# A batched long convolution with top-128 experts: other occasions for the steps of the top-k search, and a first product one occasion later

## The chip, the cores and the metric

One core of a Trainium2 chip runs the whole kernel. The metric is device microseconds of one execution, lower is better; the kernel before takes 789.25 us, the median of three runs. TensorE (PE) multiplies matrices into PSUM, VectorE (DVE), ScalarE (ACT) and GpSimd (POOL) work on SBUF and, GpSimd excepted, on PSUM, and SyncE (SP) issues most DMAs. Each engine takes its own instructions in program order and waits for the others through semaphores.

## The reference

```python
# x: (8, 6336, 128), h: (6336, 128), w_gate: (128,), w1: (128, 1024), w2: (1024, 128), capacity = 128
L = 2 * S                                   # S = 6336, a full linear convolution along S
Xf = np.fft.rfft(x, n=L, axis=1)
Hf = np.fft.rfft(h, n=L, axis=0)
y = np.fft.irfft(Xf * Hf[None], n=L, axis=1)[:, :S, :]

scores = np.einsum('bsd,d->bs', y, w_gate)
out = y.copy()
for b in range(8):
    top = np.argpartition(-scores[b], 128)[:128]
    xe = y[b, top]
    ye = np.maximum(xe @ w1, 0.0) @ w2
    g = 1.0 / (1.0 + np.exp(-scores[b, top]))
    out[b, top] = y[b, top] + g[:, None] * ye
```

So there are two parts: a convolution of every channel over the sequence, and for each of the 8 batch rows the 128 positions with the largest score, to which a gated two-layer network is added.

## The kernel before

The convolution is a discrete Fourier transform written as matrix products. The work is cut into eight units (0 to 7); units 0 to 5 go in pairs (0/1, 2/3, 4/5), each unit of a pair holding half of the channels of two batch rows, and units 6 and 7 hold one batch row each. A unit passes four stages, and TensorE does the products of each:

- **a** (16 half blocks, `stage_a`, products at L194): the first transform of x, from blocks that a fold has prepared (L133, L134, on VectorE or GpSimd). ScalarE copies the results out (L211).
- **b** (13 steps, `stage_b`, products at L109): the second transform; VectorE multiplies the result twice by the filter's spectrum into place and into a tile `tx` (L276, L282), and GpSimd adds the halves (L287).
- **c** (16 steps, `stage_c`, products at L300): the first inverse transform, copied out by ScalarE (L301).
- **d** (8 steps, `stage_d`, products at L320), the last stage: the second inverse transform. ScalarE copies one half into a tile `st` (L324), VectorE makes the sums and differences there (L329, L330), GpSimd multiplies by the gate's weights into a tile `tm` (L338), VectorE reduces `tm` to scores (L356) and SyncE sends `st` to DRAM (L359). The last two belong to `rest`, which is issued one d step later.

Stage d's products go to three PSUM banks in turn, two a step, and stage c's to the same three.

The program is a list of steps, `plan`, written out in Python with no loop on the chip. Stretches of two kinds follow each other. In a **middle stretch** stage c of unit u alternates with stage b of unit u+1, two steps of each in turn. In a **last-stage stretch** stage a of unit u+2 alternates with stage d of unit u: a0 d0 a1 d1 ... a7 d7, eight rounds. In the profile they lie as follows (start of the stretch in us): c2/b3 266.5, a4/d2 319.1, c3/b4 348.8, a5/d3 402.4, c4/b5 431, a6/d4 483.4, c5/b6 512.6, a7/d5 566.9, c6/b7 596.9.

When both units of a pair have their scores, the 128 largest of each row have to be found. This is `search`, a generator. It first makes sortable keys in two parts (`keys`, L375 to L385; its scratch is the PSUM tile `spare`, called `pm` in the profile). Then come 11 rounds (5 for the keys' upper part, 6 for the lower). A round sets seven thresholds (L454), compares the keys with them (L464), counts (L466), and adds the counts of all partitions with a small TensorE product into `pm` (L109, `pm<-num,ones`); the next VectorE step reads the sums (L444, L446, L422) and goes on to the next thresholds. In middle stretches VectorE takes five of the seven thresholds and ScalarE the other two for each unit of the pair, as four sign operations (L470, L477); in last-stage stretches VectorE takes all seven (`share`). Between the two parts the keys are rewritten (L495 to L499). After the last round `places` finds the positions: marks on VectorE (L517 to L519), a first group of products, a copy (L549), a second group, a comparison step on VectorE (L562, L568), a third group of products, and an index step for each of the two units (L591 to L595).

A generator yields a letter for what it wants to do next: "v" or "l" for a VectorE step, "p" or "q" for products, "x" for whenever. `visit(kinds)` lets the search (`strands`) and then the place finding (`later`) go one step on if their letter is among `kinds`. These calls stand behind the steps of the plan:

- middle stretch, behind an odd b (and the last one): products ("pqx"); behind an odd c, for the first six of the eight groups: VectorE steps ("vlx").
- last-stage stretch, behind a2, a4 and a6: products; behind d0, d2 and d4: VectorE steps.

`st`, `tm`, `tx`, the comparison's `cmp` and the place finding's area `work` share five buffers of one size (`wide`, 128 x 1024 float32), taken in program order from those given back.

Of the kernel before, what the change touches and what calls it, by code (L numbers as in the profile page):

```python
# [33 lines left out]
def conv_moe(ctx, tc, x, h, w_gate, w1, w2, fa_d, wb_d, wc_d, at_d, tri_d, cst_d, outs):  # L34
# [143 lines left out]
    def products_a(unit, q, t):  # L178
        xs, es = blocks[(unit + 1) * 8 + q]
        tab = fah if unit < 0 else fa  # L180
        if (unit, q) == (1, 0):
            pt = freed[t]
        elif unit < 2:
            pt = turn(wheel)
        else:
            p = pair()
            pt = (p[:, 0:512], p[:, 512:1024], p)
        for j in range(4):
            for b in range(2):
                lanes = slice(b * 64, b * 64 + N1)  # L190
                for c in range(2):
                    w = xs[lanes, 2 * j + t, 0] if c else es[lanes, 2 * j + t]
                    o = pt[b][c * 64:c * 64 + 64, 0:400].rearrange("p (r j k) -> p r j k", r=2, j=4)[:, :, j]
                    nc.tensor.matmul(o, w, tab[lanes, c], start=True, stop=True)  # L194
        return pt

    def leave_a(unit, q, t, pt, engines):
        if unit < 0:
            dst = reg[1].rearrange("p (b r m t) -> p b r m t", b=2, r=2, t=2)[:, :, :, q * 200:q * 200 + 200, t]
        else:  # L200
            dst = reg[unit % 2].rearrange("p (h r b m t) -> p h b r m t", h=2, r=2, b=2, t=2)
            dst = dst[:, q // 4, :, :, q % 4 * 200:q % 4 * 200 + 200, t]
        if pt[2] is not None:
            ops = [(dst, pt[2].rearrange("p (b x) -> p b x", b=2)[:, :, 0:400].rearrange("p b (r m) -> p b r m", r=2))]
        else:
            ops = [(dst[:, b], pt[b][:, 0:400].rearrange("p (r m) -> p r m", r=2)) for b in range(2)]
        for e, (o, i) in zip(engines, ops):
            if e == "v":
                v.tensor_copy(out=o, in_=i)
            else:  # L210
                nc.scalar.copy(out=o, in_=i)  # L211
# [3 lines left out]
    def stage_a(unit, q, t):  # L215
        pt = products_a(unit, q, t)
        engines = "ss"
        if (unit, q) > (1, 4) and unit < 2 or unit == 0 and q > 2:
            engines = "sv" if pt[2] is None else "v" if pt[2] is pairs[0] else "s"
        held.append((unit, q, t, pt, engines))  # L220
        if unit < 2 or q != 4 or t:
            while held:
                leave_a(*held.pop(0))
# [169 lines left out]
    def search(units, paced):  # L393
# [30 lines left out]
        for part in range(2):  # L424
# [3 lines left out]
            for it in range(-1, levels[part]):  # L428
                unit = base ** (levels[part] - 1 - it)
# [31 lines left out]
                with nc.allow_low_precision("whole numbers up to 64"):  # L461
# [20 lines left out]
                    else:  # L482
                        signs()
                if paced:
                    yield "p"
                else:
                    if it >= 0:
                        lower(unit)
                    if part and it + 2 == levels[part]:
                        v.tensor_tensor(out=limits, in0=bb.broadcast_to([LN, 2]), in1=edges[0:LN], op=ALU.add)  # L490
                    if units[0] + 1 == NU:
                        mark[0] = num[0:LN, 0, 0:1]
                    yield "x"
# [283 lines left out]
    def visit(kinds="vlpqx", rest=True, of=None):  # L777
        for line in of or (strands, later, others)[:3 if rest else 2]:
            if line and asks.get(id(line), "x") in kinds:
                try:  # L780
                    asks[id(line)] = next(line[0]) or "x"
                except StopIteration:
                    line.pop(0)
                    asks.pop(id(line), None)

    def more():
        if others:
            next(others[0], None)
# [24 lines left out]
    for s in plan:  # L813
        kind, unit = s[0], s[1]
# [6 lines left out]
        if kind == "a":  # L821
            q, t = s[2:]
# [16 lines left out]
            if unit >= 2 and (q, t) == (0, 1):  # L839
                load_x(n + 7)  # L840
            if t:
                visit("pqx" if q and q % 2 == 0 else "x")
        elif kind == "j":
            c = s[2]
            if c == 6:
# [21 lines left out]
        elif kind == "b":  # L867
            stage_b(*s[1:], tabs.pop(s))
            if unit == SINGLE and s[2] in (9, 11):
                load_x((unit + 2) * 8 + s[2] // 2 + 1)  # L870
            visit("pqx" if s[2] % 2 or s[2] == 12 else "x")
        elif kind == "c":
            stage_c(*s[1:])
            i = HALVES.index(s[2] // 2 * 2)
            free = True
            if unit + 2 < NU and s[2] % 2:
                m = (unit + 3) * 8
                last = unit + 3 == NU
                for q in ((0,), () if last else (5,), (1,) if last else (6, 1), (4,), (2, 3), (), (), ())[i]:
                    load_x(m + q)  # L880
                q = (None, 0, None, None, 1, 4, 2, (3, 5))[i] if last else (None, 0, 5, 6, 1, 4, 2, 3)[i]
                free = i < 6
                for q in (q if isinstance(q, tuple) else () if q is None else (q,)):
                    fold(m + q, g if free or q == 5 else v)
            if unit + 1 == NU:
                for k in range(2):
                    if loaded[0] < 1:
                        load_w(loaded[0])
                        loaded[0] += 1
                if s[2] not in (4, 12):  # L890
                    visit("pq", False)
                    visit("vlx")
                if not later_half:
                    if count[0] < 4:
                        fetch()
                else:
                    if s[2] not in (0, 2, 8):
                        more()
                    if s[2]:
                        visit(of=(strands,))  # L900
            else:
                visit(("vlx" if free else "x") if s[2] % 2 else "x")
        elif kind == "d":
            busy[0] = unit + 1 == NU
            stage_d(*s[1:], tabs.pop(s))
            i = s[2]
            if unit + 2 < NU:
                visit("x" if i % 2 or i == 6 else "vlx")
            elif unit + 1 == NU:
                hold[0] = True  # L910
                visit()
        elif kind == "end":
            flush()
            busy[0] = False
            if unit == SINGLE:
                later_half.append(1)
                serial[0] = True
                while loaded[0] < 6:
                    load_w(loaded[0])
                    loaded[0] += 1  # L920
                others.append(experts())
            if unit >= SINGLE:
                strands.append(search([unit], False))
            elif unit % 2:
                strands.append(search([unit - 1, unit], True))
                if len(strands) == 1:
                    visit("x", False)
# [104 lines left out]
```

## Time and profile before

| | before |
| --- | --- |
| median of 3 runs (lowest, highest) | 789.25 us (788.64, 790.46) |
| the profiled execution, its span | 788.46 us, 786.7 us |
| TensorE matmul busy | 727.7 us, 93% of the span |
| TensorE weight loads busy | 631.0 us, 80% |
| VectorE busy | 632.2 us, 80% |
| GpSimd busy | 551.2 us, 70% |
| ScalarE busy | 449.7 us, 57% |
| mean granted TensorE clock | 0.991 |
| DMA | 157.64 MB, mean 200 GB/s |
| chain that ended last | PE 64%, DVE 18%, DMA 7%, issue 5%, ACT 3% |

Weight loads overlap matmuls, and matmuls are pipelined with modelled ends, so busy times of TensorE add up to a little more than its time. In the timeline rows below, the columns are start and length in us, engine, source line, operation, output and inputs with their shapes, and the count of instructions merged into the row; a bracket gives the time that the engine sat idle before the row and what ended it. Rows of one group that come from other places are parted by "...".

### The profile page before, as it was taken

The numbers are of one execution on the slowest core, as the hardware profiler recorded it, in microseconds if no ns is written. First come the engines' busy times: TensorE is split into PE (matmuls) and PEld (weight loads), VectorE is DVE, ScalarE is ACT, GpSimd is POOL, SyncE is SP. The second block draws the span as 40 slices with busy tenths as digits, with TensorE's granted clock in tenths as the row PEclk, the third lists the DMA queues.
The fourth block names the chain that finished last, engine by engine and source line by source line (L and its number), as shares of the span: only waits on it lengthen the run. The fifth ranks groups of instructions, "written<-read, shape, count | busy, mean of one in ns | idle before, by whom it ended". The sixth has DMA issues, their size and how long they took to land.

```text
span 786.7 us, 39709 instructions
## 1 busy us (share of the span) xinstructions
PE 727.7 (93%) x17566; PEld 631.0 (80%) x17566; DVE 632.2 (80%) x1070; ACT 449.7 (57%) x962; POOL 551.2 (70%) x406
## 2 busy tenths in 40 slices
PE   6799899999999999999999999999999998889565
PEld 6776688898889888888799789878988787879554
DVE  6579966767676799899777898999678997986883
ACT  5687653465346566665456566655554666666462
POOL 0039939976997599868977698767985676734823
PEclk9999999999999999999999999999999999999889
DMA  9539737567856775577647774699487846532600
GB/s 334 190 133 328 247 97 245 177 197 244 275 178 193 241 269 180 168 229 261 210 146 231 257 256 124 194 327 317 132 251 252 265 118 186 160 89 61 211 26 17
DMA packets 82293, 157.64 MB, mean 200 GB/s; under 512 B 9367, under 2 KB 30089, under 8 KB 82121
## 3 DMA queue, kind: packets, MB, share of 16 engines
q1 hardware_dynamic: 81224, 154.05, 60.7%
q8 instruction: 138, 2.26, 1.2%
q0 software_dynamic: 896, 1.05, 0.5%
q14 instruction: 35, 0.28, 0.1%
HBM read 121.77 MB, written 33.29 MB: 197 GB/s over the span
## 4 chain that ended last, share of the span: by engine, by line
PE 64%; DVE 18%; DMA 7%; issue 5%; ACT 3%; POOL 1%; SPq 1%; POOLq 0%; DVEq 0%; ACTq 0%
PE pb L300 22%; PE pt L109 17%; PE pt L194 10%; PE pb L320 10%; DMA out<-st 3%; DVE cmp L464 2%; PE pb L109 2%; ACT junk L477 2%; PE pb L194 2%; DVE tx L282 2%; DVE st L329 2%; DVE st L330 1%; DVE ss L354 1%; PE pm L109 1%; POOL tm L338 1%
## 5 line engine op out<-in xcount | busy, mean ns | idle before, releaser
L301 ACT COPY half<-pb 114x512 f32<-114x512 f32 x224 | 146.8, 655 | 166.0 <-PE pb L300 165.6
L287 POOL TENSOR_TENSOR big<-big,tx 128x512 f32<-128x512 f32 (+1 forms) x104 | 132.1, 1300 | 72.9 <-DVE tx L282 63.0
L338 POOL TENSOR_TENSOR tm<-st,wg 114x1024 f32<-114x1024 f32 x56 | 133.8, 2392 | 60.6 <-DVE st L330 41.9
L287 POOL TENSOR_TENSOR reg<-reg,tx 128x512 f32<-128x512 f32 (+1 forms) x104 | 130.9, 1292 | 43.8 <-PE pb L300 22.6
L300 PE MATMUL pb<-wc,reg 128*50 128x64 f32 x4096 | 123.1, 220 | 1.9 <-ACT st L324 1.9
L300 PEld LDWEIGHTS pb<-wc,reg 128*50 128x50 f32 x4096 | 119.2, 126 | 5.3 <-ACT st L324 2.6
L300 PEld LDWEIGHTS pb<-wc,big 128*50 128x50 f32 x4096 | 118.7, 126 | 3.0 <-ACT reg L211 0.2
L300 PE MATMUL pb<-wc,big 128*50 128x64 f32 x4096 | 120.9, 219 | 0.1
L320 PE MATMUL pb<-half,wbuf 114*50 114x128 f32 x1792 | 110.5, 273 | 3.3 <-DMA wbuf<-tab_at 1.4
L320 PEld LDWEIGHTS pb<-half,wbuf 114*50 114x50 f32 x1792 | 96.1, 122 | 9.5 <-DMA wbuf<-tab_at 1.6
L109 PE MATMUL pt<-big,wbuf 128*64 128x256 f32 x704 | 86.0, 388 | 0.1
L109 PE MATMUL pt<-reg,wbuf 128*64 128x256 f32 x704 | 85.1, 388 | 0.0
L211 ACT COPY reg<-pt 128x800 f32<-128x800 f32 x66 | 58.1, 929 | 37.4 <-PE pt L194 35.7
L282 DVE TENSOR_TENSOR tx<-pt,wbuf 128x1024 f32<-128x1024 f32 (+1 forms) x65 | 76.3, 1174 | 0.0
L329 DVE TENSOR_TENSOR st<-pb,st 114x512 f32<-114x512 f32 x56 | 38.6, 689 | 43.7 <-PE pb L320 29.2
L109 PEld LDWEIGHTS pt<-big,wbuf 128*64 128x64 f32 x704 | 51.1, 135 | 23.9 <-DVE tx L282 0.6
L109 PEld LDWEIGHTS pt<-reg,wbuf 128*64 128x64 f32 x704 | 53.1, 135 | 20.1
L356 DVE TENSOR_REDUCE ss<-tm 114x16 f32<-114x1024 f32 x48 | 58.4, 1216 | 7.9 <-POOL tm L338 7.4
L211 ACT COPY big<-pt 128x800 f32<-128x800 f32 x56 | 49.2, 934 | 24.6 <-PE pt L194 22.7
L194 PE MATMUL pt<-fa,big 50*64 50x100 f32 x2336 | 60.5, 250 | 1.0 <-issue 0.7
L282 DVE TENSOR_TENSOR reg<-pt,wbuf 128x1024 f32<-128x1024 f32 (+1 forms) x39 | 45.9, 1178 | 18.8 <-PE pt L109 18.5
L194 PEld LDWEIGHTS pt<-fa,big 50*64 50x64 f32 x2336 | 52.4, 133 | 7.8 <-issue 4.9
(177 smaller groups left out, 1197.9 us busy)
## 6 DMA issues: line engine op xcount, KB each, us to landing
wbuf<-tab_at SPq DMA_DIRECT2D x128, 200.0 KB
out<-st SPq DMA_DIRECT2D x112, 200.0 KB
wbuf<-tab_wb SPq DMA_DIRECT2D x84, 256.0 KB
wbuf<-hd SPq DMA_DIRECT2D x84, 256.0 KB
big<-in_x SPq DMA_DIRECT2D x37, 512.0 KB
half<-in_x SPq DMA_DIRECT2D x15, 512.0 KB
hd<-st SPq DMA_DIRECT2D x24, 256.0 KB
reg<-in_x SPq DMA_DIRECT2D x12, 512.0 KB
```

Of the source, the lines that this page charges most:

```text
L109: nc.tensor.matmul(out[lo:hi], w[:, lo:hi], r, **k)
L194: nc.tensor.matmul(o, w, tab[lanes, c], start=True, stop=True)
L211: nc.scalar.copy(out=o, in_=i)
L282: v.tensor_tensor(out=dst.rearrange("p h a j k t -> p k h a j t"), in0=src, in1=w, op=ALU.mult)
L287: g.tensor_tensor(out=yv[:, :, r], in0=yv[:, :, r], in1=zv[:, :, 1 - r], op=ALU.add if r else ALU.subtract)
L300: nc.tensor.matmul(pt[i2 * 64:i2 * 64 + N1, o:o + HD], w, wc[:, i2], start=True, stop=True)
L301: nc.scalar.copy(out=hv[0:LN, c * 4 + j:c * 4 + j + 2].rearrange("p j r m t -> p (j r) t m"), in_=pt[0:LN].rearrange("p (j t m) -> p j t m ...
L320: nc.tensor.matmul(pt[r][a * 64:a * 64 + N1, c * 128:c * 128 + 128], ats[c // 2][0:LN, c % 2, a, r], hv[0:LN, :, r, m], start=True, stop=True)
L329: v.tensor_tensor(out=st[:, 0:512], in0=pt[1][0:LN], in1=st[:, 512:1024], op=ALU.add)
L338: e.tensor_tensor(out=tm[:, o:o + z].rearrange("p (a d) -> p a d", d=n), in0=st[:, o:o + z].rearrange("p (a d) -> p a d", d=n), in1=w.unsq ...
L356: v.tensor_reduce(out=ss[u][:, :, :, 4 * i:4 * i + 4].rearrange("p b s c -> p s c b"), in_=tm.rearrange("p (s c b d) -> p s c b d", s=2, c ...
L464: v.tensor_tensor(out=cv, in0=cur.unsqueeze(2).broadcast_to([LN, nb, nv, HD]), in1=nth[:, :, 0:nv].unsqueeze(3).broadcast_to([LN, nb, nv, ...
```

## The change

The change touches four places. The condition in `stage_a` is rewritten. The search yields "p" once more, and so lets one occasion for a product pass, between its first comparison and its first product, for pairs 0/1 and 2/3 (`units[0] < 4`). The last-stage stretches offer other occasions: products behind a1, a4 and a7 in place of a2, a4 and a6, and VectorE steps behind d1 and d4 in place of d0, d2 and d4.

```diff
@@ stage_a
-        if (unit, q) > (1, 4) and unit < 2 or unit == 0 and q > 2:
+        if unit == 0 and q > 2 or unit == 1 and q > 4:
             engines = "sv" if pt[2] is None else "v" if pt[2] is pairs[0] else "s"
@@ search
                 if paced:
+                    if it < 0 and not part and units[0] < 4:
+                        yield "p"
                     yield "p"
@@ the plan's loop, stage a
             if t:
-                visit("pqx" if q and q % 2 == 0 else "x")
+                visit("pqx" if q in (1, 4, 7) else "x")
@@ the plan's loop, stage d
             if unit + 2 < NU:
-                visit("x" if i % 2 or i == 6 else "vlx")
+                visit("vlx" if i in (1, 4) else "x")
```

Followed through the plan, the steps of pair 0/1 come at these places (pair 2/3 does the same two units later, pair 4/5's own steps stay where they are):

| stretch | before | with the change |
| --- | --- | --- |
| c2/b3 | keys; comparisons 1 to 5; products 1 to 5, from b3 on | keys; comparisons 1 to 4; products 1 to 4, from b5 on |
| a4/d2 | d0: count and key rewrite; d2: comparison 6; a4: product 6; d4: count and comparison 7; a6: product 7 | d1: count and comparison 5; a4: product 5; d4: count and key rewrite |
| c3/b4 | comparisons 8 to 11, products 8 to 11; marks; first and second products of the place finding | comparisons 6 to 11, products 6 to 11 |
| a5/d3 | d0: comparison step; a2: third products; d2, d4: index steps | d1: last count and marks; a4: first products; d4: copy; a7: second products |
| c4/b5 | | c5: comparison step; b1: third products; c7, c13: index steps |

In the last row the search of pair 2/3 begins in the same stretch; for pair 2/3 that row is c6/b7, where the search of pair 4/5 begins.

## Rows read from the trace of the kernel before

**Rows 1.** Busy time by stretch: length, then busy us (instructions) of each engine, clock, DMA
```profile
158.60:186.30 27.70, 27.70 (x774) 25.30 (x776) 18.68 (x22) 19.07 (x25) 20.30 (x12) 1.00 0.71 215
...
319.10:348.80 29.70, 27.91 (x778) 25.43 (x780) 26.37 (x39) 18.90 (x25) 21.80 (x12) 1.00 0.69 207
```

**Rows 2.** Timeline, TensorE, search products: start, length, form, [idle before <-releaser]
```profile
281.79 0.20 PE L109 MATMUL pm<-num,ones 114*64 114x14 bf16 x2 [0.82 <-ACT junk L477]
...
343.38 0.20 PE L109 MATMUL pm<-num,ones 114*64 114x14 bf16 x2 [1.34 <-DVE num L466]
...
446.12 0.19 PE L109 MATMUL pm<-num,ones 114*64 114x14 bf16 x2 [0.86 <-ACT junk L477]
...
499.22 0.20 PE L109 MATMUL pm<-num,ones 114*64 114x14 bf16 x2 [0.53 <-DVE num L466]
...
507.18 0.19 PE L109 MATMUL pm<-num,ones 114*64 114x14 bf16 x2 [1.01 <-DVE num L466]
...
612.49 0.19 PE L109 MATMUL pm<-num,ones 114*64 114x14 bf16 x2 [1.12 <-ACT junk L477]
...
619.75 0.17 PE L109 MATMUL pm<-num,ones 114*64 114x14 bf16 x1
```

**Rows 3.** Timeline, VectorE, search operations inside the stretch of Rows 1's second row
```profile
323.96 0.17 DVE L444 TENSOR_TENSOR ge<-pm,least 114x14 f32<-114x14 f32 x1
...
324.88 1.72 DVE L497 TENSOR_SCALAR key<-key 114x128 f32<-114x128 f32 x1
326.63 0.23 DVE L498 TENSOR_SCALAR key<-key 114x128 f32<-114x128 f32 x1
...
327.11 0.68 DVE L329 TENSOR_TENSOR st<-pb,st 114x512 f32<-114x512 f32 x1
...
340.31 0.16 DVE L444 TENSOR_TENSOR ge<-pm,least 114x14 f32<-114x14 f32 x1
```

**Rows 4.** Timeline, GpSimd, the same stretch
```profile
328.64 4.85 POOL L338 TENSOR_TENSOR tm<-st,wg 114x1024 f32<-114x1024 f32 x2 [2.12 <-issue]
333.45 1.27 POOL L133 TENSOR_TENSOR big<-big 128x512 f32<-128x512 f32 x1
```

**Rows 5.** Timeline, TensorE and then VectorE, start of the stretch after 430.8 us
```profile
434.25 3.80 PE L109 MATMUL pt<-reg,wbuf 128*64 128x256 f32 x32
...
434.92 1.22 DVE L356 TENSOR_REDUCE ss<-tm 114x16 f32<-114x1024 f32 x1 [1.43 <-POOL tm L338]
...
437.83 0.43 DVE L385 TENSOR_TENSOR key<-pm,cst 114x256 f32<-114x256 int32 x1
```

**Rows 6.** Timeline, VectorE and then TensorE, place finding in the stretch 402 to 431
```profile
407.55 1.28 DVE L562 TENSOR_TENSOR work<-tri,pm 114x512 bf16<-114x512 f32 x2
408.75 0.75 DVE L568 SCALAR_TENSOR_TENSOR work<-pm,work 114x256 bf16<-114x256 f32 x2
...
416.83 0.15 DVE L591 TENSOR_SCALAR base<-pm 128x1 f32<-128x1 f32 x1
...
417.59 0.68 DVE L329 TENSOR_TENSOR st<-pb,st 114x512 f32<-114x512 f32 x1
...
411.00 0.29 PE L109 MATMUL pm<-lanes,work 114*64 114x1 bf16 x8
...
411.52 1.94 PE L320 MATMUL pb<-half,wbuf 114*50 114x128 f32 x32
```

**Rows 7.** Timeline, VectorE, one round of the stretch 597 to 650
```profile
630.35 0.16 DVE L444 TENSOR_TENSOR ge<-pm,least 114x14 f32<-114x14 f32 x1
...
632.82 0.68 DVE L276 TENSOR_TENSOR reg<-pt,wbuf 128x512 f32<-128x512 f32 x1
...
637.60 0.16 DVE L444 TENSOR_TENSOR ge<-pm,least 114x14 f32<-114x14 f32 x1
```

**Rows 8.** Timeline, ScalarE and then SyncE's queue, stretch 402 to 431
```profile
413.75 0.59 ACT L324 COPY st<-pb 114x512 f32<-114x512 f32 x1 [1.57 <-DMA out<-st]
...
407.94 1.69 SPq L359 DMA_DIRECT2D out<-st  x2
```

## The prediction

> **What bounds the kernel now.** I read the stretch table first. The middle of the kernel (158 to 650 us) repeats two kinds of stretch: last-stage stretches (first products of one unit beside the sums and output of another, eight rounds) and middle stretches (stages b and c). Where no search runs, TensorE is busy for the whole stretch, 27.70 of 27.70 us, which makes a round 3.46 us; the clock is full in both rows [rows 1]. So TensorE is the bound, and any other engine matters only where TensorE waits for it. With search steps beside it the same stretch takes 29.70 us, with TensorE busy for 27.91 and VectorE up from 18.68 to 26.37 [rows 1]. Then I listed TensorE's instructions and looked for idle brackets. Each pair's search has 11 counting products; [rows 2] has seven of the three pairs', six with an idle bracket. Two kinds: beside the last stage they wait for VectorE's counts (1.34, 0.53, 1.01 us), and the first one after a pair's keys waits for ScalarE's signs (0.82, 0.86, and 1.12 for the third pair) [rows 2]. All of it is 5.7 us, 0.7% of the span; a few smaller waits are left as they are. That is the purse the change can pay from.
>
> **The change, part by part.** The condition on `engines` is rewritten, and selects the same units and blocks: nothing. The rest moves steps; the number of products, counts and place-finding products is the same, so TensorE's own work is left out of the sum wherever it stands. For pairs 0/1 and 2/3 the last-stage stretch held three VectorE steps after d0, d2, d4 and products at a4, a6; it then holds two, after d1 and d4, and one product, at a4. What no longer fits moves on: six search rounds instead of four in the next middle stretch, place finding (marks, first and second products) beside the following last stage, and its third products and index steps into the middle stretch after that, where the next pair's search starts.
>
> (1) First product of pair 0/1, one occasion (7 us) later: its signs are long done, -0.8 us [rows 2].
>
> (2) First product of pair 2/3: -0.9 us [rows 2]. But the third products of pair 0/1 now stand just before it, after the second b. They write the bank in which the keys' halves lie, so they wait until VectorE has read those. The keys' last operation starts at 437.83 and lasts 0.43, TensorE's second b ends at about 437.9 (434.25 + 3.80, less the overlap of ends), so the bare wait is some 0.3 us [rows 5]. VectorE gets the comparison step of place finding (1.28 + 0.75 = 2.0 us) [rows 6] ahead of that, where it idled 1.43 us for GpSimd [rows 5], so the keys end some 0.65 us later: wait +0.95. Net +0.1; bounds -0.6 (wait 0.3) and +0.5.
>
> (3) Beside the last stage, twice. The waits of 1.34 and of 0.53 + 1.01 go: -2.9 us [rows 2]. What is late next is VectorE itself. A step with its count takes 3.0 us (from 340.31 until the product at 343.38) [rows 2, 3], a round's own VectorE work is two sums of 0.68 and a reduction of 1.2 [rows 3, 5]. Counted from the end E1 of d1 on TensorE: 0.2 of latency, sums, reduction and step end at E1+5.7, so d2's sums end at E1+7.1 instead of E1+5.0. GpSimd's multiply of d2 (2.42, half of 4.85) then ends at E1+9.5, the fold queued behind it (two operations of 1.3) at E1+12.1, the multiply of d3 at E1+14.5, which is E4+4.1 [rows 4]. The reduction of d3 waits for that, and the second step stands behind the reduction: it starts at E4+5.3. It contains the key rewrite, 3.15 us in all (323.96 to 327.11) [rows 3], so d5's sums end at E4+8.7 to +9.9. TensorE's d7 needs the bank that they free at E4+8.45, and the next stage's first and third blocks need the banks of d6 and d7. VectorE has 5.1 us more to do until the last of them, at E4+13.8 to +15.0, and TensorE wants it at E4+12.2. That makes 1.6 to 2.8 us of wait in each stretch; if d3's reduction isn't held up it is none. I take 1.5 each, +3.0, so part (3) is +0.1; bounds -2.9 and +2.7.
>
> What the rewrite costs decides within that. One of its operations takes 1.72 us and the next, of the same form, 0.23 [rows 3]. [...]
>
> (4) Start of pair 4/5's search, from 597 us. Its first product isn't moved, and the comparison step, third products and both index steps of pair 2/3 now come into it. There VectorE has no room: a round is a step of 2.47 and products of 4.78, together 7.25 [rows 7], which is TensorE's round too (612.49 to 619.75, and the second product has no wait) [rows 2]. An index step is 0.76 [rows 6]. Two of them and the 0.65 of part (2) put the third product 2.2 us later. TensorE fills 0.5 of that with the moved third products themselves (411.00 to 411.52) [rows 6], which are not counted: +1.65. Bounds +0.6 (the wait for the keys hides one index step) and +2.0.
>
> (5) Buffers. Outputs, products, comparisons and the place-finding work area share five buffers, taken in the order in which they were given back. The work area held one over d0 to d2 in the stretch shown; it then holds one from d1 until the next middle stretch. Where four were left, ScalarE's copy of d2 waited 1.57 us for the output of d0 to land, 5.8 us after its issue at 407.94 [rows 8]. A buffer then takes copy and sums 2.1 (0.59 + 2 x 0.68, issue), transfer 5.8, so 7.9 per two rounds of 6.9: up to 1 us of lag more every second round. TensorE first waits when the copy is some 2.8 us late (the bank that it frees is used again 0.95 into the next sums), which d6 or d7 could just reach. I take +0.5 in each of two stretches, nearest to the one row that shows no cost on TensorE, +1.0; bounds 0 and +4.
>
> (6) One comparison a pair goes from seven thresholds on VectorE to five there and four signs on ScalarE: nothing, since only a search's first product waits for signs there and the moved one is not a first [rows 2]; without that cover up to 1.1 us a pair, the largest such wait [rows 2]. No DMA is issued by a moved step, so SyncE's and GpSimd's queues keep their order.
>
> Sum: -0.8 + 0.1 + 0.1 + 1.65 + 1.0 = **+2.0 us**. The profiled execution took 788.46 us with a span of 786.7, so it would take 790.5. The median of the three runs shown is 0.8 above the profiled one, so the predicted time is 789.25 + 2.0 = 791.3 us.
>
> **Rivals.** *Buffers in full*: part (5) reaches +4. For it: the lag grows by itself once it starts; against it: only one copy in the row's stretch waited, and buffers may be handed over in a kinder order. 794.3 us. *Faster, the last stage runs clear*: with two steps in place of three VectorE has 3 us less to do there. If the step after d1 ends before GpSimd is pushed behind its fold, d3's reduction isn't held, no bank is late and outputs leave early enough for four buffers: parts (3) and (5) lose 3.0 and 1.0, 787.3 us. It decides at E1+5.0, the time at which d2's sums end undisturbed. For it: VectorE's total there falls below eight rounds; against it: the step is 3.0 us in one piece. *VectorE absorbs the index steps*, and buffers cost nothing: -1.65 - 1.0, 788.6 us; against it the 7.25 of 7.25. *It does not do what it says*: waits move without a net effect, 789.3 us.
>
> **How the numbers follow.** Chances: forecast 0.40 (own range 789.9 to 792.7), buffers in full 0.15, last stage clear 0.17, index steps absorbed 0.18, no effect 0.10. A difference of 0.2% (1.6 us) is about what a measurement of this kernel can tell from none, so the borders are 787.7 and 790.8. Faster: 0.17 and 0.02 of the absorbed case, 0.19. Same: the rest of that, 0.16, no effect 0.10, and 0.07 of the forecast below 790.8: 0.33. Slower: 0.33 + 0.15 = 0.48. The range runs from the clear case to the full buffers, 787.3 to 794.5.
>
> **What would show it.** Right: no idle bracket before the pair's first products; no product waiting beside the last stage, but waits of 0.2 to 1.5 us before the last sums there and the first blocks of the next stage; a wait of about 1 us before each group of third products; second and third products of pair 4/5 waiting 0.7 us each. It is wrong if VectorE is idle before the sums of d5, if the multiply of d3 starts on time, or if pair 4/5's products run without waits. Instruction fetch gaps on TensorE (0.3 to 0.5 us each, in stretches without search too) are left as they are; moved, they could shift the time by about as much.

## The result, and the profile after

The changed kernel takes 796.7 us, the median of 22 runs (792.0 to 802.3); the kernel before took 791.5 beside it (22 runs, 788.6 to 796.2), 2.3 us more than in the three runs known ahead. The ratio is 1.0055 (95% interval 1.0033 to 1.0078): slower by 4.4 us (2.6 to 6.2; the two medians lie 5.2 apart). The forecast was +2.0.

The profiled execution has a span of 794.1 us, 7.4 more than before. That is more than the medians differ, since the profiled execution of before (788.46) lies 3.1 us below the median of its 22 runs and that of after (795.91) 0.8 below its own. The stretch table shows where the 7.4 are: five stretches of before and then of after (c2/b3, a4/d2, c4/b5, a7/d5, c6/b7; length, then busy us and instructions of TensorE, its weight loads, VectorE, ScalarE, GpSimd, then clock, DMA share, GB/s).

```profile
266.30:319.00 52.70, 51.88 (x1240) 45.24 (x1234) 49.09 (x67) 30.08 (x77) 45.41 (x36) 1.00 0.67 218
319.00:348.50 29.50, 27.71 (x773) 25.22 (x772) 26.47 (x39) 18.84 (x25) 21.61 (x12) 1.00 0.69 206
430.60:483.40 52.80, 51.94 (x1244) 45.34 (x1238) 49.17 (x67) 30.04 (x76) 45.75 (x36) 1.00 0.67 220
566.80:596.67 29.87, 28.33 (x800) 25.60 (x800) 19.93 (x33) 18.99 (x25) 24.11 (x14) 1.00 0.69 211
596.67:650.50 53.83, 52.00 (x1241) 43.92 (x1237) 50.28 (x100) 30.77 (x78) 34.17 (x28) 1.00 0.68 213
```

```profile
266.80:318.40 51.60, 51.60 (x1238) 43.00 (x1232) 46.82 (x61) 28.17 (x67) 44.32 (x35) 1.00 0.66 218
318.40:346.70 28.30, 27.70 (x775) 25.04 (x771) 21.35 (x34) 19.09 (x25) 21.28 (x12) 1.00 0.68 206
428.60:483.90 55.30, 53.09 (x1274) 45.81 (x1268) 51.14 (x74) 28.85 (x69) 47.38 (x36) 1.00 0.64 208
566.30:597.73 31.43, 29.13 (x798) 26.14 (x798) 19.17 (x29) 18.43 (x24) 24.01 (x15) 1.00 0.64 195
597.73:657.30 59.57, 54.89 (x1272) 44.97 (x1268) 54.02 (x113) 31.10 (x78) 35.12 (x28) 0.97 0.62 195
```

The change gains where it takes steps away (c2/b3 -1.1, a4/d2 -1.2, with VectorE at 21.35 us there for 26.47) and loses where they go: c4/b5 +2.5, a7/d5 +1.6, and above all c6/b7, +5.7, where the clock's mean is 0.97.

At the start of c4/b5, TensorE's timeline (start, length, form, in brackets the idle time ahead and what ended it) shows two blocks of stage c waiting for the last stage's banks, and then the third products of pair 0/1 waiting for pair 2/3's keys:

```profile
428.68 1.06 PE L300 MATMUL pb<-wc,big 128*50 128x64 f32 x32
430.77 1.10 PE L300 MATMUL pb<-wc,big 128*50 128x64 f32 x32 [1.02 <-ACT st L324]
432.22 2.00 PE L300 MATMUL pb<-wc,big 128*50 128x64 f32 x64 [0.34 <-DVE st L330]
434.05 3.80 PE L109 MATMUL pt<-reg,wbuf 128*64 128x256 f32 x32
438.44 0.29 PE L109 MATMUL pm<-lanes,work 114*64 114x1 bf16 x8 [0.60 <-DVE key L385]
```

Inside c6/b7 the same two waits stand again, for pairs 2/3 and 4/5, and then comes a gap that no other engine ends:

```profile
599.64 1.10 PE L300 MATMUL pb<-wc,big 128*50 128x64 f32 x32 [0.75 <-ACT st L324]
601.09 2.00 PE L300 MATMUL pb<-wc,big 128*50 128x64 f32 x64 [0.34 <-DVE st L330]
...
607.32 0.29 PE L109 MATMUL pm<-lanes,work 114*64 114x1 bf16 x8 [0.61 <-DVE key L385]
...
613.26 0.55 PE L300 MATMUL pb<-wc,big 128*50 128x64 f32 x13 [2.01 <-issue]
613.64 3.40 PE L109 MATMUL pt<-reg,wbuf 128*64 128x256 f32 x16
...
618.88 0.17 PE L109 MATMUL pm<-num,ones 114*64 114x14 bf16 x2
```

"issue" means that TensorE waited for nothing that the profile shows. Behind it 16 products of stage b take 3.40 us in place of 2.0. The table of these microseconds shows two things: the DMA engines are full until 614 (a share of 1.04), and the granted clock is 0.50 from 614 to 616, after TensorE stood still for 2.01 us.

```profile
610.00:612.00 2.00, 1.24 (x45) 1.13 (x41) 2.00 (x4) 1.20 (x2) 2.00 (x2) 1.00 1.04 386
612.00:614.00 2.00, 0.74 (x17) 0.66 (x18) 1.89 (x5) 0.15 (x1) 2.00 (x3) 0.97 1.04 385
614.00:616.00 2.00, 2.00 (x14) 1.05 (x12) 0.82 (x5) 1.87 (x8) 0.81 (x1) 0.50 0.44 159
616.00:618.00 2.00, 2.00 (x16) 1.17 (x14) 0.92 (x2) 0.44 (x2) 0.00 (x0) 0.68 0.01 5
```

TensorE's instructions come by DMA too. The page's queue list (queue, kind, packets, MB, share) has

```profile
q8 instruction: 138, 2.26, 1.2%
```

and 2.26 MB in 138 packets are 16.4 KB each, which for 2 x 17566 products and weight loads is one packet for about 255 instructions. The places of the gaps give the size too. Counted in order of start, TensorE's semaphore instructions among them, the gaps marked "issue" after 100 us stand at instructions 3521, 3777, 11458, 11714 and 15298 in the profile of before, and at 3521, 3777, 11714, 21954, 23490 and 28865 in that of after: multiples of 256 apart, to within one. So one fetch brings a block of 256. Most borders between blocks show no gap: of the 126 packets of q8 that land after 99 us in each of the two profiles, only 5 and 6 are followed by such a gap; the one in the timeline above is 2.01 us.

That such a gap is a late fetch can be read from the trace. One packet of q8 runs from 610.83 to 612.03, the first since 603.04, and TensorE goes on at 613.26, 1.23 us after it has landed. All 11 gaps marked "issue" on TensorE after 100 us, in the profiles of both kernels, end 1.23 to 1.58 us after a packet of q8 has landed; in the runs below, gaps with this mark are counted as late fetches. The packet before the gap took 1.20 us, against a median of 1.07 for q8 in this execution: it was not slow, it came late.

The new steps beside the last stage ran as the prediction had them. VectorE and GpSimd in a4/d2 (timeline; the brackets as above), then TensorE at its end:

```profile
326.86 1.21 DVE L356 TENSOR_REDUCE ss<-tm 114x16 f32<-114x1024 f32 x1
...
339.87 1.22 DVE L356 TENSOR_REDUCE ss<-tm 114x16 f32<-114x1024 f32 x1 [2.29 <-POOL tm L338]
341.01 0.16 DVE L444 TENSOR_TENSOR ge<-pm,least 114x14 f32<-114x14 f32 x1
...
341.93 0.35 DVE L499 TENSOR_SCALAR key<-key 114x128 f32<-114x128 f32 x1
342.32 0.23 DVE L500 TENSOR_SCALAR key<-key 114x128 f32<-114x128 f32 x1
342.58 0.29 DVE L501 TENSOR_TENSOR key<-key 114x128 f32<-114x128 f32 x1
342.79 0.68 DVE L329 TENSOR_TENSOR st<-pb,st 114x512 f32<-114x512 f32 x1
```

```profile
334.84 1.29 POOL L133 TENSOR_TENSOR big<-big 128x512 f32<-128x512 f32 x1
336.20 1.29 POOL L134 TENSOR_TENSOR big<-big 128x512 f32<-128x512 f32 x1
337.45 4.75 POOL L338 TENSOR_TENSOR tm<-st,wg 114x1024 f32<-114x1024 f32 x2
```

```profile
346.69 2.00 PE L300 MATMUL pb<-wc,reg 128*50 128x64 f32 x64 [0.49 <-DVE st L330]
349.35 2.00 PE L300 MATMUL pb<-wc,reg 128*50 128x64 f32 x64 [0.66 <-DVE st L330]
```

No product of the search waits in a4/d2 or a6/d4 any more, against 2.9 us in [rows 2].

### The profile page after: what moved, and what is told of

The parts are those of the page before. It is cut to its first block, busy times and chain, and to the rows that moved or that the text cites. A ratio compares the mean times of both kernels' runs of the same rounds, so it can differ in the third digit from the quotient of the medians.

```text
span 794.1 us, 39720 instructions
## 1 busy us (share of the span) xinstructions
PE 732.3 (92%) x17566; PEld 629.8 (79%) x17566; DVE 628.0 (79%) x1070; ACT 453.3 (57%) x980; POOL 551.6 (69%) x406
## 3 DMA queue, kind: packets, MB, share of 16 engines
q8 instruction: 138, 2.26, 1.2%
## 4 chain that ended last, share of the span: by engine, by line
PE 64%; DVE 21%; issue 6%; DMA 5%; ACT 3%; SPq 1%; POOL 1%; POOLq 0%; DVEq 0%; ACTq 0%
PE pb L300 21%; PE pt L109 17%; PE pt L194 11%; PE pb L320 10%; DMA out<-st 3%; DVE cmp L464 2%; DVE tx L276 2%; PE pb L109 2%; PE pb L194 1%; DVE ss L354 1%; DVE st L329 1%; DVE st L330 1%; PE pm L109 1%; DVE big L276 1%; DVE tx L282 1%
## 5 line engine op out<-in xcount | busy, mean ns | idle before, releaser
L338 POOL TENSOR_TENSOR tm<-st,wg 114x1024 f32<-114x1024 f32 x56 | 133.8, 2393 | 63.5 <-DVE st L330 52.8
L109 PEld LDWEIGHTS pt<-reg,wbuf 128*64 128x64 f32 x704 | 50.6, 136 | 23.5 <-issue 1.0
```

The costliest lines, as they stand in the source:

```text
L109: nc.tensor.matmul(out[lo:hi], w[:, lo:hi], r, **k)
L338: e.tensor_tensor(out=tm[:, o:o + z].rearrange("p (a d) -> p a d", d=n), in0=st[:, o:o + z].rearrange("p (a d) -> p a d", d=n), in1=w.unsq ...
```

## The experiments

What had to be told apart: are the 4.4 us the waits that the prediction summed (buffers, keys, index steps), or the late instructions? Each run stands beside the kernel before on the same chip; its ratio is given with the 95% interval. Diffs are against the changed kernel unless said otherwise.

**Each pair alone.** The first-pair run keeps the old occasions for units 6 and 7 of stage a:

```diff
-visit("pqx" if q in (1, 4, 7) else "x")
+visit("pqx" if q in ((1, 4, 7) if unit < 6 else (2, 4, 6)) else "x")
-visit("vlx" if i in (1, 4) else "x")
+visit("vlx" if i in ((1, 4) if unit < 4 else (0, 2, 4)) else "x")
-if it < 0 and not part and units[0] < 4:
+if it < 0 and not part and units[0] < 2:
```

> The change for pair 0/1 alone: new occasions in the last-stage stretches a4/d2 and a5/d3 and the later first product for that pair; pair 2/3 keeps the old ones, so pair 4/5's search starts as in the kernel before. Theory A (the loss sits where pair 4/5's search starts, c6/b7, which took 59.5 us in place of 53.7, and in the stretch ahead of it, 31.5 in place of 30.0): no loss, ratio to before 0.998 to 1.001, c6/b7 53 to 55 us, and no gap of 2 us between TensorE's instructions there. Rival B (each pair pays by itself, for its keys, its index steps and its buffers): about half of the 4.4 us, ratio 1.002 to 1.004, seen in c4/b5 (52.7 before, 55.2 after).

The second-pair run has the conditions the other way round (unit > 5, unit > 3, units[0] == 2).

> The change for pair 2/3 alone: new occasions in a6/d4 and a7/d5 and the later first product for that pair; pair 0/1 as in the kernel before. Theory A: the whole loss, ratio 1.005 to 1.008, with c6/b7 57 to 60 us and a gap between TensorE's instructions of 1 to 2 us in it. Rival B: the other half, ratio 1.002 to 1.004, c6/b7 55 to 56 us.

Measured: 1.0037 (1.0009 to 1.0064) and 1.0034 (1.0003 to 1.0065). Both ratios lie in the ranges of rival B, by which each pair pays for itself, though the second's interval reaches into theory A's range too. With the first pair alone c4/b5 takes 56.7 us (before 52.8) and c6/b7 53.8 as before; with the second, c6/b7 takes 59.9 and has a gap of 2.29 us at the place of the 2.01:

```profile
617.02 0.49 PE L300 MATMUL pb<-wc,big 128*50 128x64 f32 x10 [2.29 <-issue]
```

So the gap comes in two kernels, and theory A's place is right, but its claim that nothing is lost elsewhere is not. That it comes in every execution isn't shown: one of each was profiled, and this one (799.87 us) is the slowest of its 12 runs.

**Moving the stream.** Products of one column at the very start, where TensorE waits for its first data (5.22 us in the kernel before), move every later block border:

```diff
+for _ in range(64):
+    nc.tensor.matmul(spare[0:64, 0:1], ones16[:, 0:64], ones16[:, 0:1], start=True, stop=True)
```

> The changed kernel with 64 products of one column at its very start, where TensorE waits for the first blocks: its 128 instructions move the rest of TensorE's stream by half of the 256 instructions that one fetch brings (16384 bytes each in the trace). Theory A (fetches are late because the DMA queues are full of outputs and tables there): a fetch falls elsewhere, but the place stays full; the ratio stays 1.004 to 1.008 and c6/b7 stays above 57 us. Rival C (the gap of 2.01 us at 613.26 and the half clock after it are an accident of where the blocks of 256 end): the gap is gone there, c6/b7 is 54.5 to 56 us and the ratio 0.999 to 1.003.

> The kernel before with the same 64 products at its start. Theory A: ratio 0.998 to 1.002, no gap of over 1 us after the first 106 us. Rival C: the time moves by 2 us or more either way, by gaps at other places than the 0.28, 0.45 and 0.45 us that the kernel before shows after 106 us; a gap of over 1 us in a middle stretch would show that any kernel can meet one.

With 32 of them in the changed kernel:

> The changed kernel with 32 products of one column at its start: 64 instructions, a quarter of what one fetch brings. If the place where a fetch falls decides on the gap of 2.01 us in c6/b7, it is smaller (0 to 1.5 us) or at another place of the stretch, and the ratio is 1.001 to 1.005; if the full DMA queues alone decide, it is there with 1.5 to 2.5 us, ratio 1.004 to 1.008.

Measured: 1.0014 (0.9984 to 1.0043) with 64, 1.0024 (0.9995 to 1.0052) with 32, and the kernel before with 64 0.9996 (0.9969 to 1.0023). The gap is gone in both shifted runs; c6/b7 takes 56.4 and 57.2 us. So the place of the border has a part in it, as rival C said. And where the gap is gone, the prediction's own waits come out; the run with 32, TensorE in c6/b7:

```profile
601.01 1.98 PE L109 MATMUL pt<-reg,wbuf 128*64 128x256 f32 x16
...
605.41 0.29 PE L109 MATMUL pm<-lanes,work 114*64 114x1 bf16 x8 [0.60 <-DVE key L385]
...
613.49 0.19 PE L109 MATMUL pm<-num,ones 114*64 114x14 bf16 x2 [0.17 <-ACT junk L477]
...
621.52 0.20 PE L109 MATMUL pm<-num,ones 114*64 114x14 bf16 x2 [0.59 <-ACT junk L477]
...
629.54 0.19 PE L109 MATMUL pm<-num,ones 114*64 114x14 bf16 x2 [0.60 <-ACT junk L477]
```

The 0.60 and the two waits of pair 4/5's second and third products (0.59, 0.60; forecast 0.7 each) stand where part (4) put them. In the unshifted kernel the gap had given VectorE that time.

**Old occasions for place finding.** In a5/d3 and a7/d5 only, so that the third products come back beside the last stage:

```diff
+visit("pqx" if q in ((2, 4, 6) if unit % 2 else (1, 4, 7)) else "x")
+visit("vlx" if i in ((0, 2, 4) if unit % 2 else (1, 4)) else "x")
```

In this run the next pair's keys overwrite what the second index step reads, so the places of units 1 and 3 are not the reference's; the work is the same.

> The changed kernel with the old occasions in a5/d3 and a7/d5 (steps after d0, d2, d4, products at a2, a4, a6) and the new ones in a4/d2 and a6/d4. The third products and the comparison step of place finding come back beside the last stage, so the keys' bank is not waited for, and the work area goes back to the ring before the next middle stretch; the index steps still stand in c4/b5 and c6/b7. Rival K (the tail of place finding in the middle stretches carries the loss): the two waits of 0.6 us on the keys and most of those for buffers at the start of c4/b5 and c6/b7 (1.36 and 1.09 us) go, the gap of 2 us too since the stream ahead of it is another; the gains stay, ratio to the kernel before 0.996 to 0.999. Theory A (VectorE has no room beside the last stage for five steps): a5/d3 and a7/d5 grow by 1.5 to 3 us each, ratio 1.000 to 1.004.

Then with both index steps in one visit ahead of the keys, which makes it a whole kernel again:

```diff
-            if j:
+            if j and units[0] > 3:
                 yield "l"
```

> As the run with the old occasions in a5/d3 and a7/d5, but both index steps of pairs 0/1 and 2/3 in one visit, ahead of the next pair's keys, so that the places are the reference's. Theory (that run's 0.9996 came from gains in a4/d2, a6/d4, c2/b3 and c4/b5 of 1.0 + 1.3 + 0.5 + 0.8 = 3.6 us against a5/d3 and a7/d5 at +1.1 and +1.3 or more): ratio 0.997 to 1.001; the second index step (0.76 us) delays pair 4/5's first product by 0 to 0.8 us more than its 1.1. Rival (VectorE's work ahead of the keys is on the path twice): ratio 1.001 to 1.004, with waits of 1.5 us or more at the first products in c4/b5 and c6/b7.

Measured: 0.9996 (0.9971 to 1.0021) and 0.9992 (0.9970 to 1.0014). The first ratio lies between the ranges of the two theories, and the profiles show something of both. Rival K, by which the loss is the tail of place finding in the next middle stretch, has its signs: in the second run c4/b5 takes 52.0 us and TensorE waits for nothing at its start; of c6/b7 only the first product's wait of [rows 2] is left, and VectorE's second index step costs it nothing:

```profile
610.87 0.19 PE L109 MATMUL pm<-num,ones 114*64 114x14 bf16 x2 [1.14 <-ACT junk L477]
```

Theory A has the longer last-stage stretches: a5/d3 (29.3) and a7/d5 (32.4) are longer by 1.0 and 2.5, and so the order doesn't beat the kernel before by more than the measurement can tell.

**Room for the buffers.** The products `tm` in bf16 in two buffers of their own, and four for the rest, in the changed kernel and in the kernel before:

```diff
-tp.tile([128, 1024], F32, tag="t", name=name, bufs=5)
+tp.tile([128, 1024], F32, tag="t", name=name, bufs=4)
-wide("tm")[0:LN]
+tp.tile([128, 1024], BF16, tag="tm", name="tm", bufs=2)[0:LN]
```

> The changed kernel with two buffers of their own for the products of the gating weights (written in bf16, so keys and places are not the reference's; the number of steps is the same), and four buffers for the rest: in effect six in place of five. To be set against the kernel before with the same edit. Rival D (the shared buffers carry the loss, by outputs that leave late): the waits of 1.0 and 0.3 us at the start of c4/b5 and c6/b7 go, the difference between the two is 1.5 us or less, and the gap of 2 us in c6/b7 goes with them since the outputs leave earlier. Theory A (keys, index steps and the late instructions): the difference stays at 3 to 5 us.

> The kernel before with the same two bf16 buffers beside four. Both theories: within 2 us of the kernel before (ratio 0.997 to 1.002), since only one copy per stretch waited there for a buffer and TensorE for none.

Measured: 1.0021 (0.9987 to 1.0054) and 1.0009 (0.9972 to 1.0046): 1.0 us apart in place of 4.4, with wide intervals. What TensorE waits for at the start of c4/b5 and c6/b7 tells more. In the changed kernel four of ScalarE's copies in a7/d5 wait for outputs to leave, as this one (1.57 for one copy in [rows 8]), and the next stretch begins with 1.09 us of waits (599.64 and 601.09 above):

```profile
591.34 0.59 ACT L324 COPY st<-pb 114x512 f32<-114x512 f32 x1 [1.82 <-DMA out<-st]
```

With room, the list of TensorE's waits in c6/b7 (us in total, times, longest) has neither of the two, and the gap is 1.3:

```profile
PE pb L300 <- issue: 1.3, 1, 1.3
PE pb L320 <- ACT half L301: 0.7, 1, 0.7
PE pm L109 <- DVE key L385: 0.6, 1, 0.6
PE pm L109 <- ACT junk L477: 0.6, 1, 0.6
```

So the waits at the start of c4/b5 and c6/b7 (1.02 + 0.34 and 0.75 + 0.34) are the buffers'. The room doesn't touch the wait for the keys (0.6), and the gap, forecast to go with the buffers, only shrinks.

**Third products one occasion later**, alone and with the room:

```diff
         yield "q"
+        if units[0] < 4:
+            yield "q"
         pls = []
```

> The changed kernel with the third products one occasion later, behind a product of the next pair and so clear of the keys. Sum of waits: the two of 0.6 us on the keys go, the buffers' 2.4 us stay; -1.2 us against the changed kernel, ratio to the kernel before 1.002 to 1.005, or 1.000 to 1.003 if the gap of 2 us in c6/b7 goes as well, since its stream is another ahead of that place. Rival K (the place finding's tail is the cause of all that follows): the buffers' waits are still there but the ratio falls to 0.999 to 1.001.

> Both at once: two bf16 buffers of their own for the gating products (keys and places are not the reference's) and the third products one occasion later. If the waits add up, the 2.4 us for buffers and the 1.2 us for keys are gone together and the gains of 1.0 + 1.3 + 0.8 + 0.5 us remain: ratio to the kernel before 0.996 to 1.000, 1 to 3 us below the run with the buffers alone. If the late instructions decide, a gap of over 1 us stays in c6/b7 and the ratio is 1.001 to 1.004.

Measured: 1.0078 (1.0050 to 1.0107) and 1.0003 (0.9977 to 1.0029). The second lies 0.0003 above the range for the sum of waits and, as that sum had it, 1.4 us below the room alone; it has no gap over 1 us. The first (7 runs) is a miss of both theories: the waits on the keys and the gap are gone in its profile, as expected, but pair 4/5's first product waits 1.26 again, TensorE waits 1.62 in c4/b5 for a copy that waits for an output to leave, and the ratio is above the changed kernel's, though the intervals overlap. Its profiled span, 792.0, is at the low end of its own spans (791.1 to 799.0), so the profile doesn't show what made it slow.

**Without the outputs.** Unit 5's last three rounds send nothing; other numbers are written there earlier:

```diff
-for a in range(2):
+for a in range(0 if unit == 5 and i > 4 else 2):
```

> The changed kernel without the outputs of the last three rounds of unit 5 at their place (a7/d5); other numbers are written there some 50 us earlier, so this part of the output is not the reference's. TensorE's instructions are the same. Theory A (the gap of 2.01 us in c6/b7 comes from fetches that are late because the DMA queues are full): the DMA share 8 to 16 us into c6/b7 falls from 1.0 to 0.7 to 0.9, the gap to under 0.7 us, c6/b7 from 59.5 to 55 to 57 us and the ratio to 1.000 to 1.004. Rival C (the place of the block's end alone decides): the gap stays 1.5 to 2.3 us, c6/b7 57 us or more, ratio 1.003 to 1.008.

Measured: 1.0101 (1.0062 to 1.0140, 6 runs), which says nothing, since the earlier writes delay the tables of c5/b6 (62.7 us, 5.9 us of waits for the second transform's tables, `tab_wb`). The stretch c6/b7 does: same TensorE instructions, no gap, c6/b7 55.7 us, and this where the gap was (12 to 16 us into it):

```profile
621.00:623.00 2.00, 2.00 (x28) 1.47 (x24) 1.89 (x6) 0.78 (x3) 2.00 (x2) 1.00 0.93 313
623.00:625.00 2.00, 1.88 (x18) 1.05 (x15) 1.93 (x7) 1.86 (x9) 1.48 (x2) 1.00 0.77 228
```

With the shifted runs it makes two conditions: moving the border took the gap away, and so did thinning the traffic (DMA share 0.93 and 0.77 where it had been 1.04), each seen in one profiled execution a run. The queues were still full in the run with 32 products (1.02 in the row below) with no gap, so there full queues alone made none.

```profile
608.00:610.00 2.00, 2.00 (x67) 1.87 (x64) 2.00 (x4) 1.56 (x3) 2.00 (x2) 1.00 1.02 365
```

**Four streams moved by 64 instructions**, and the controls. Each has the loop above with range(32) in it, the last one with range(96):

> The third products one occasion later, and 32 products of one column at the very start (64 instructions). Theory F (the place of the stream at which a fetch falls decides on the rest of the loss): ratio 1.000 to 1.004, that is 3 us or more below the same kernel without them (1.0078). Rival (the order of the steps itself costs it, by waits): 1.005 to 1.010, with the same waits before the products of pair 4/5 (2.3 us) and for a buffer in c4/b5 (1.6 us).

> The change for pair 2/3 alone with the 64 instructions at the start. Theory F: the gap of 2.29 us in c6/b7 is gone, c6/b7 56 to 57.5 us in place of 59.9, ratio 0.999 to 1.002 in place of 1.0034. Rival: the gap or one of its size stays somewhere in c6/b7, ratio 1.002 to 1.005.

> The change for pair 0/1 alone with the 64 instructions at the start. Theory F: only a gap of 0.7 us in c4/b5 is there to lose, ratio 1.001 to 1.004 (1.0037 without them), the buffers' 1.5 us and the keys' 0.6 us in c4/b5 stay. Rival: a lucky shift helps every order alike by 2 to 3 us, ratio 0.998 to 1.001.

> Both index steps in one visit and place finding at the old occasions, with the 64 instructions at the start. Theory F: nothing to gain, ratio 0.997 to 1.002 (0.9992 without them). Rival: a lucky shift helps every order alike, ratio 0.994 to 0.998.

> The kernel before with 32 products of one column at its start. Theory G (these 64 instructions shorten the start of any order, by 2 us): ratio 0.996 to 0.999, first 106.8 us shortened to 104.5 to 106, the other stretches as before. Theory F (only the streams of the changed orders lie badly): ratio 0.999 to 1.001.

> The changed kernel with 96 products of one column at its start (192 instructions). If the gap of 2.01 us belongs to the first place of the stream alone: none above 0.7 us in c6/b7, ratio 1.001 to 1.004, less by 0.002 if the start gains as with 32. If any place meets one sooner or later: a gap of 1 to 2.5 us in one of the middle stretches, ratio 1.004 to 1.007.

| | not moved | moved by 64 instructions |
| --- | --- | --- |
| kernel before | 1 | 0.9996 (0.9965 to 1.0027) |
| changed kernel | 1.0055 (1.0033 to 1.0078) | 1.0024 (0.9995 to 1.0052) |
| third products later | 1.0078 (1.0050 to 1.0107) | 1.0030 (1.0009 to 1.0050) |
| second pair alone | 1.0034 (1.0003 to 1.0065) | 1.0020 (0.9999 to 1.0041) |
| first pair alone | 1.0037 (1.0009 to 1.0064) | 0.9977 (0.9954 to 1.0000) |
| both index steps together | 0.9992 (0.9970 to 1.0014) | 0.9977 (0.9950 to 1.0003) |

The changed kernel with 96 products (192 instructions): 1.0034 (1.0002 to 1.0067), gaps of 0.6 and 0.5 us in c6/b7, none larger. The kernel before doesn't care; all five changed orders become faster, by 0.14 to 0.60%. The two intervals of the first pair don't overlap and those of the third products just touch; the other three overlap, and their evidence is that all point one way. Theory F said that of the orders with a gap, and the second pair's gap went (c6/b7 56.4). But the first pair alone, which had no gap over 0.7 us after the first stretches, gained most and lies below theory F's range and its rival's, and theory G falls with the kernel before.

The late fetches explain a part. Summed behind the first 107 us of the profile, in us not moved and moved, they are 1.2 and 1.2 for the kernel before, 3.5 and 2.1 for the changed kernel, 4.5 and 1.6 for the second pair, 2.5 and 0 for the first pair, 1.4 and 1.2 for both index steps together, but 2.1 and 2.7 for the third products later, which gained 0.48%. So small gaps add up: for the first pair they make 2.5 of its 4.7 us (0.60%). Where the rest sits is open: c4/b5 is as long in both (56.7, 56.5), and the rest is spread over stretches that also differ between executions of one kernel.

## Why the prediction was right or wrong

The sign was right; the size (+4.4 for +2.0) was not, and 796.7 lies above the range. 2.3 us of the 5.4 between 791.3 and 796.7 are the level of the kernel before, which three runs had put too low.

With the stream at three other places the change costs 1.0014, 1.0024 and 1.0034, on average 1.0024; the kernel before stands at 0.9996 at two. That is +2.2 us, the size of the forecast. The changed kernel's own place costs 0.3% more; by the intervals this is an estimate of 0.31 with 0.28 either way, so just clear of the noise.

The step that failed is the last sentence of "What would show it": gaps in instruction fetch of 0.3 to 0.5 us, "left as they are", that might shift the time by about as much. They were sized by the gaps that the kernel before happens to have, and stood in the sum with nothing. In the profiled execution the gap was 2.01 us, and the stretch at the lower clock behind it (0.50, then 0.68) cost another 1.6 (16 products in 3.40 and 16 in 2.22 in place of 2.0 each): 3.6 of the 5.7 us of c6/b7. How often it comes in the 22 runs isn't shown, and so what share of the lasting 0.3% it makes stays open. The lower clock is at most a small part of the lasting loss: the mean granted clock over the timed runs is 0.9852 for the changed kernel (22 runs) and 0.9860 for the kernel before (35), and 0.0008 of 794 us is some 0.6 us, an estimate.

A second step was mis-sized, and another hid it. Part (5) put the buffers at +1.0, and they cost the profiled execution 3.3; part (3), at +0.1, came to -1.5. So that the average of +2.2 meets the forecast's +2.0 is partly luck.

The terms follow, by the profile of after and, where named, of the runs. A bracket shows a little less than a wait costs. In the run with 32 products the two counting rounds with brackets of 0.59 and 0.60 take 8.03 and 8.02 us (613.49 to 621.52 to 629.54); without a bracket a round takes 7.26 (612.49 to 619.75 [rows 2]). So each wait costs some 0.17 us more than its bracket.

- Part (1), -0.8: right. c2/b3 is 1.1 us shorter, with no wait at the first product.
- Part (2), +0.1: the third products wait 0.60 for the keys (438.44 above), not 0.95, and the first product's 0.86 is gone: -0.3.
- Part (3), +0.1: the chain held to a tenth of a microsecond (second step forecast at E4 + 5.3 = 341.0, as E4, the end of d4 on TensorE, is 335.7; it starts at 341.01), and the waits came before the next stage's first blocks: 0.49 + 0.66 in c3/b4. But in c5/b6 only 0.25, so 1.4 for the two, not 3.0. What was mis-sized is the key rewrite, 3.15 us in [rows 3] and 1.8 here (341.01 to 342.79): its first long operation took 0.35, not 1.72. It began at 341.93, and GpSimd's multiplies ended at 337.45 + 4.75 = 342.20, so it met the last 0.3 us of one. In the kernel before it began at 324.88, 0.76 us into a multiply that ran to 326.52 (row below). In both kernels, and in pair 2/3's rewrites too (1.73 before, 0.34 after), it ended 0.08 us after the multiply did. Why the two end together isn't shown; the prediction took the 1.72 of the one case for the size of any. Net -1.5.
- Part (4), +1.65: right, wherever the gap is gone. In the run with 32 products the brackets are 0.60 + 0.17 + 0.59 + 0.60 in place of 1.12 [rows 2], +0.84. The delay itself is larger: from the stretch's first product of stage b to the third counting product it is 28.53 us (601.01 to 629.54), and 26.65 in the kernel before (rows below). Of the +1.88, 0.5 are the moved third products themselves, which the part doesn't count: +1.4. In the unshifted kernel only one wait of 0.26 is left, since the gap gave VectorE the time.
- Part (5), +1.0: right as a mechanism, too small for this stream. The brackets are 1.36 and 1.09, together 2.45, and nothing with the room. From the start of c4/b5 to its first product of stage b it is 5.37 us (428.68 to 434.05), and 3.57 before (430.68 to 434.25); in c6/b7 5.08 (597.84 to 602.92) and 3.58: together +3.3. In the shifted runs the brackets are 0.5 (64 products), 1.6 (32) and 1.0 (96).
- Part (6), nothing: right, but not for its reason. It said that only a search's first product waits for signs in these stretches; the second product of c3/b4 waits 0.47 for them before and 0.49 after (rows below), and that of c5/b6 0.45 in both.
- Not in the sum: the tables of a7/d5 are waited for 1.02 + 1.28 us, before 1.41. Also TensorE's gaps behind the first stretch, 3.5 us against 1.2; 2.01 of them are the one gap.

The rows for parts (3) and (4), of the kernel before, and for part (6), of the kernel before and then of after:

```profile
324.12 2.40 POOL L338 TENSOR_TENSOR tm<-st,wg 114x1024 f32<-114x1024 f32 x1 [1.66 <-DVE ge L444]
```

```profile
600.36 1.99 PE L109 MATMUL pt<-reg,wbuf 128*64 128x256 f32 x16
...
627.01 0.18 PE L109 MATMUL pm<-num,ones 114*64 114x14 bf16 x2
```

```profile
363.74 0.20 PE L109 MATMUL pm<-num,ones 114*64 114x14 bf16 x2 [0.47 <-ACT junk L477]
...
362.72 0.20 PE L109 MATMUL pm<-num,ones 114*64 114x14 bf16 x2 [0.49 <-ACT junk L477]
```

Of the rivals, buffers in full (+4) came to 3.3. The last stage did run nearly clear, as that rival said, but its condition, that d3's reduction isn't held, failed (2.29 us idle at 339.87): what spared the time was the short rewrite. VectorE did not absorb the index steps where the gap is gone (0.59 and 0.60 above).

## What to carry to other kernels

Before moving a step into a stretch, look at what its buffers and banks hold there: here the third products that wait for another search's keys (0.60 and 0.61 us) and the work area that keeps a buffer through the outputs (3.3) cost the profiled execution more than the waits that the move took away (2.9 beside the last stage, of which 1.4 came back, and 0.82 and 0.86 at the first products). And a difference of half a per cent between two orders of one kernel should be measured with the instruction stream at several places, by a few idle instructions at the start, before it is put down to the order.

## What the runs showed that was not expected

- A fetch of TensorE's instructions came late by 2.01 us in the changed kernel, with the DMA engines' share at 1.04. Gaps with the same mark in c6/b7 were 2.29 us in the second pair alone, 1.3 when the outputs left earlier, 0.6 and 0.5 with the stream moved by 192 instructions; there was none with it moved by 64 or 128, or without the outputs.
- 64 idle instructions at the start changed five orders of this kernel by 0.14 to 0.60% and the kernel before by 0.04%. Only a part of this could be tied to late fetches.
- After the stand of 2.01 us the granted clock was 0.50 from 614 to 616 and 0.68 from 616 to 618; after stands of 1.0 to 1.3 us in a7/d5 of the same execution it stayed at 1.00.
